# From unit 4 on, V is the stationary operand and P, divided by its sums first, the moving one

## Chip, cores and metric

One core of a Trainium2 chip. The metric is device time in microseconds (us), the median over runs of the whole kernel. Engines: PE is TensorE (PEld its weight load, which overlaps), DVE VectorE, ACT ScalarE, POOL GpSimd, SP the queue that issues nearly all DMAs.

## What is computed

Attention over 4 batches, 8 heads, 768 positions of 64 values, with a bias by head, in which a row sees the first `n_global` columns and the `n_local` before it. Its output, 3072 rows of 512, goes through a feed-forward layer of 2048 (512 to 2048 to 512).

```python
scores = scale * q @ k.T + bias          # bias = -slope[head] * distance
a = exp(where(keep, scores, -1e9) - max)
a = a / (sum(a) + 1e-9)
x = a @ v                                # heads side by side: 3072 x 512
h = x @ w_in
g = maximum(h, 0) + alpha * minimum(h, 0)
out = g @ w_out
```

## The kernel before

The work is cut into 12 units (`NU`) of 256 positions, three to a batch, `c = u % 3` being the place in the batch; each unit has two tiles of 128 rows, `t`. A row sees at most 192 kept columns (its own 128 and the ones before, or the first 32), held in 64-column groups `g`; for the first unit of a batch (`c = 0`) one group of tile 0 is missing ("gap").

From unit 2 on, products in fp16 are made of a high and a low half, three products for one. For one head:

- `split_pair` (L756) loads q and k of two heads and splits them; `load_pair` (L772) puts the score products of two heads in one PE operation, of four heads (`wide = 4`) from unit 4 (`QUAD`) on, in the PSUM buffers sp and av. They are products of 64 rows by 64 columns of the array, four of which stand side by side (`scores_of`, L687).
- `attend` (L803): DVE adds the bias and takes the maximum (L831), ACT takes the exponential and its row sums (L843), POOL and DVE form the sums' inverse for a group of `GROUP[u]` heads (L856, L859). P, not yet divided, is scaled and split into ps, high half on ACT (L385, by `mul`), low half on DVE (L412, by `rest`), each for all 384 columns at once; SP transposes it by DMA into pt (L890).
- `values` (L906): P transposed is the stationary operand, V the moving one, 64x64 by 64 columns; 36 such products a head (27 where `c = 0`), all heads of a group in one PE operation (L925). The result, rows by head columns in PSUM, is multiplied by the inverse sums on DVE into xn (L936).
- `pieces` (L941), from unit 4 on: three sums and differences of quarters of xn (L953), a high and a low half of each piece in xs (L397, L411), and four DMA transposes on SP into xt (L967). `seven` (L1074) makes the hidden layer of two blocks from seven products instead of eight (L1108); `ff_out` (L1154) makes the output products (L1170). Units 0 to 3 use `ff_in` (L1010) with whole weights.

All operations go to `Plan` (L150) with a key, the place in a common order (16 keys to a unit from unit 2 on), and estimated costs; a list scheduler picks for each engine the ready operation of lowest key, and the order it finds is the program's. So each engine works in a fixed order, and PE waits at an operation until every operand of it is there. The constants at L314 to L363 set keys (`LEAD`: how many keys ahead of its hidden layer a unit's attention begins; `F1`, `W0`: first loads), estimated costs (`SLOW`, `SHARE`, `BLOCK`) and buffer counts (`sp=2, av=2, h=2, o=2` are the eight PSUM banks).

Of the kernel before, what the change touches and what calls it, by code (L numbers as in the profile page):

```python
# [15 lines left out]
F16 = mybir.dt.float16  # L16
# [8 lines left out]
P = 128  # L25
# [22 lines left out]
def lay_out(q, k, v, n_global, n_local, moe_w_in, moe_w_out, moe_alpha):  # L48
# [5 lines left out]
    qk = np.zeros((NU, 4, P, 672), q.dtype)  # L54
    for u in range(NU):
        b, c = divmod(u, 3)
        cols = list(range(256 * c, 256 * c + 128)) + list(range(GL))
        cols += list(range(256 * c + 128, 256 * c + 256))
        if c:
            cols = list(range(256 * c - LOC, 256 * c)) + list(range(GL)) + cols  # L60
        n = 256 + len(cols)
        both = np.concatenate([qt[b, :, :, 256 * c : 256 * c + 256], kt[b][:, :, cols]], axis=2)
        qk[u, :, :, :n] = both.transpose(1, 0, 2).reshape(4, P, n)

    def groups(u, which):
# [3 lines left out]
        for t in range(2):  # L69
            at = 256 * c + 128 * t  # L70
            sets = (range(at - LOC, at - GL), list(range(at - GL, at)) + list(range(GL)), range(at, at + 64),
                    range(at + 64, at + 128))
            for n, g in enumerate(which):
                if at or g > 1:
                    out[64 * t : 64 * t + 64, n] = vn[b][list(sets[g])]
# [16 lines left out]
            [qk[0, :, :, :544], v0[:, :, 2:].reshape(P, 4, 260).transpose(1, 0, 2)], axis=2),  # L92
        "in_far0_dram": cont(v0[64:, :, :2].reshape(64, 2, 520).transpose(1, 0, 2)),
        "in_qk_dram": cont(qk[1:]),
        "in_first1v_dram": cont(groups(1, range(4)).transpose(0, 2, 1, 3).reshape(P, 2, 1024).transpose(1, 0, 2)),
        "in_far2_dram": cont(groups(2, (0, 1)).reshape(P, 1024)),
        "in_own_dram": cont(np.stack([groups(u, (2, 3)).reshape(P, 1024) for u in range(NU)])),
# [218 lines left out]
LEAD = 22  # L316
# [5 lines left out]
DP = 3.5  # L322
FLEX = {'ACT': 1.5, 'DVE': 2, 'POOL': 1}
GROUP = (4, 4, 2, 4, 4)
# [13 lines left out]
F1, F1S, W0, W0S = -60, 1, -61, 2  # L338
# [13 lines left out]
SHARE = 0.25  # L352
SLOW, SLOWER = 1.09, 1.04
V1S, V1M, V1R = 5.5, 2.5, 1
STEP4 = 1.5
# [10 lines left out]
def fast(tc, cn, a):  # L366
    nc = tc.nc
    ctx = ExitStack()
    with ctx:
# [64 lines left out]
        def build_bias(key):  # L434
# [7 lines left out]
            def columns():  # L442
                kw = dict(allow_small_or_imprecise_dtypes=True)
                nc.gpsimd.iota(rel.t[:, 0:LOC], pattern=[[-1, LOC]], base=LOC, channel_multiplier=1, **kw)
                nc.gpsimd.iota(rel.t[:, LOC:P], pattern=[[0, GL]], base=0, channel_multiplier=0, **kw)
                nc.gpsimd.iota(rel.t[:, P : 2 * P], pattern=[[-1, P]], base=0, channel_multiplier=1, **kw)
                nc.gpsimd.iota(j.t[:, 0:P], pattern=[[1, P]], base=0, channel_multiplier=0, **kw)

                nc.gpsimd.affine_select(out=rel.t[:, P : 2 * P], in_=rel.t[:, P : 2 * P], pattern=[[-1, P]],
# [967 lines left out]
```

## Time and profile before

| | |
|---|---|
| median of 3 runs | 609.06 us (605.25 to 611.16) |
| profiled execution | 601.96 us |
| its span | 600.2 us |
| mean granted clock of TensorE | 0.995 |
| PE busy | 570.6 us (95%) |
| DVE busy | 481.7 us (80%) |
| ACT busy | 406.9 us (68%) |
| POOL busy | 78.6 us (13%) |

The profile is one execution. The span is from its first to its last instruction. Busy times overlap across engines; a wait is put down to the operand that came last, and "issue" means that the engine waited for nothing that the profile shows. A wait that names an engine long done was for another thing, often a DMA.

### The profile page before, as it was taken

The page shows a single profiled execution, that of the slowest core. Times are in us where ns is not written, and L with a number is a line of the kernel's source. Part 1 is how long each engine was busy: PE and PEld are TensorE (multiplying, and loading weights), DVE is VectorE, ACT ScalarE, POOL GpSimd, SP SyncE. Part 2 cuts the span into 40 slices and gives each one's busy share as a digit, 9 for nine tenths or more (in the row PEclk, how much of TensorE's full clock was granted, in tenths as well). Part 3 has the DMA queues.
Part 4 walks back from the last instruction along what each step waited for, and adds up shares of the span by engine and source line. Part 5 has one row for each costly group of instructions (what it writes and reads, how often), then busy time and mean ns, then how long its engine had stood idle before and what let it go on. Part 6 is the DMA issues. An engine that isn't in the chain of part 4 may idle for free.

```text
span 600.2 us, 21524 instructions
## 1 busy us (share of the span) xinstructions
PE 570.6 (95%) x8844; PEld 408.7 (68%) x8844; DVE 481.7 (80%) x1368; ACT 406.9 (68%) x1053; POOL 78.6 (13%) x161
## 2 busy tenths in 40 slices
PE   7789999999999998989999898999999989989995
PEld 5667666666667676767767676777777767767783
DVE  6899999998896896789699497799698778676532
ACT  7899999988797689468477378577467556431321
POOL 2002333333333330000000000001000001000000
PEclk9899999999999999999999999999999999999999
DMA  8995786265565597498798697589798684422001
GB/s 277 409 406 205 195 224 195 44 133 141 118 142 108 133 250 166 101 192 175 183 181 185 134 202 140 119 207 182 157 212 132 128 189 67 90 43 24 36 2 41
DMA packets 123962, 94.04 MB, mean 157 GB/s; under 512 B 101712, under 2 KB 102480, under 8 KB 123856
## 3 DMA queue, kind: packets, MB, share of 16 engines
q1 hardware_dynamic: 123712, 92.46, 65.1%
q8 instruction: 71, 1.16, 0.8%
q14 instruction: 35, 0.29, 0.2%
q10 hardware_dynamic: 144, 0.13, 0.1%
HBM read 58.22 MB, written 6.29 MB: 107 GB/s over the span
## 4 chain that ended last, share of the span: by engine, by line
PE 76%; DVE 10%; DMA 7%; issue 3%; ACT 2%; SPq 1%; POOL 0%; DVEq 0%; ACTq 0%; POOLq 0%
PE o L1170 35%; PE ha L1108 13%; PE hc L1108 10%; PE h L1020 9%; PE av L918 5%; PE sp L696 3%; DMA xt<-xs 3%; DMA w<-in_w_dram 1%; DMA pt<-ps 1%; DMA first<-in_qk_dram 1%; DVE whl L412 1%; DVE pr L831 1%; DMA first<-in_first_dram 1%; DVE wf L604 1%; DVE g L1033 1%
## 5 line engine op out<-in xcount | busy, mean ns | idle before, releaser
L1170 PE MATMUL o<-whl,gh 128*128 128x512 f16 (+1 forms) x800 | 230.2, 371 | 0.0
L1170 PE MATMUL o<-whl,gl 128*128 128x512 f16 (+1 forms) x400 | 148.2, 371 | 1.9 <-DVE vdg L521 1.5
L1170 PEld LDWEIGHTS <-gh 128*128 128x128 f16 x800 | 71.6, 98 | 52.4 <-issue 2.3
L1108 PEld LDWEIGHTS <-sw 128*128 128x128 f16 x1536 | 91.5, 98 | 20.5 <-issue 7.3
L1020 PE MATMUL h<-xt,whl 128*128 128x256 f16 x768 | 92.3, 273 | 1.6 <-DVE g L1033 1.5
L1020 PEld LDWEIGHTS <-whl 128*128 128x128 f16 x768 | 74.4, 98 | 20.1 <-issue 2.6
L843 ACT ACTIVATE pr<-pr,sm 128x192 f32<-128x192 f32 (+1 forms) x176 | 77.1, 441 | 7.6 <-DVE sm L831 7.4
L1108 PEld LDWEIGHTS <-whl 128*128 128x128 f16 x1152 | 70.9, 98 | 14.0
L1170 PEld LDWEIGHTS <-gl 128*128 128x128 f16 x400 | 39.1, 98 | 45.2 <-DVE gl L1037 0.9
L411 POOL TENSOR_TENSOR gl<-g,gh 128x256 f16<-128x256 f32 x58 | 51.7, 892 | 115.0 <-ACT gh L1035 88.9
L831 DVE CUSTOM_DVE_ANT_0 pr<-sp,D 128x192 f32<-128x192 f32 (+1 forms) x192 | 58.6, 340 | 2.8 <-PE sp L696 2.5
L1108 PE MATMUL hc<-xt,sw 128*128 128x128 f16 x768 | 53.4, 219 | 4.3 <-DVE ga L1119 2.2
L1108 PE MATMUL ha<-xt,sw 128*128 128x128 f16 x768 | 53.4, 219 | 0.4 <-ACT u L1115 0.4
L1108 PE MATMUL ha<-xt,whl 128*128 128x128 f16 x768 | 53.3, 219 | 0.0
L412 DVE SCALAR_TENSOR_TENSOR ps<-pr,ps 128x384 f16<-128x384 f32 (+1 forms) x80 | 43.5, 544 | 6.9 <-ACT ps L385 6.7
L385 ACT ACTIVATE gh<-ga 128x512 f16<-128x512 f32 x32 | 20.2, 630 | 37.9 <-DVE ga L1147 37.8
L385 ACT ACTIVATE ps<-pr 128x384 f16<-128x384 f32 (+1 forms) x78 | 38.9, 502 | 2.5 <-DMA pt<-ps 2.3
L851 POOL TENSOR_TENSOR fin<-fin,sm 128x8 f32<-128x8 f32 (+1 forms) x22 | 8.4, 381 | 219.9 <-ACT pr L843 218.3
L385 ACT ACTIVATE g<-h,ak 128x256 f32<-128x256 f32 x59 | 27.6, 469 | 13.5 <-PE h L1020 9.4
L1115 ACT COPY u<-ha 128x256 f32<-128x256 f32 x32 | 11.8, 369 | 34.0 <-DVE ga L1119 33.7
L843 ACT ACTIVATION_READ_ACCUMULATOR pr<-pr,sm 128x1 f32 x176 | 33.8, 192 | 0.0
L412 DVE SCALAR_TENSOR_TENSOR x<-raw,x 128x672 f16<-128x672 f32 (+1 forms) x40 | 33.5, 843 | 0.0
(152 smaller groups left out, 930.8 us busy)
## 6 DMA issues: line engine op xcount, KB each, us to landing
w<-in_w_dram SPq DMA_DIRECT2D x32, 512.0 KB, 8.5
again<-in_w_dram SPq DMA_DIRECT2D x32, 512.0 KB, 4.8
raw<-in_qk_dram SPq DMA_DIRECT2D x28, 336.0 KB, 3.4
out_dram<-os SPq DMA_DIRECT2D x23, 256.0 KB, 2.6
rawv<-in_own_dram SPq DMA_DIRECT2D x10, 512.0 KB, 4.7
raw<-in_qk_dram SPq DMA_DIRECT2D x12, 272.0 KB, 3.6
gp<-v SPq DMA_DIRECT2D x48, 64.0 KB, 2.2
vr<-in_own_dram SPq DMA_DIRECT2D x3, 512.0 KB, 5.2
```

The costliest lines, as they stand in the source:

```text
L385: lambda: nc.scalar.mul(out=out(), in_=src(), mul=by.t if tile_ else by)),
L411: return e.tensor_tensor(out=out(), in0=src(), in1=hi(), op=ALU.subtract)
L412: return e.scalar_tensor_tensor(out=out(), in0=src(), scalar=val(), in1=hi(), op0=ALU.mult, op1=ALU.subtract)
L696: nc.tensor.matmul(out[i].t[64 * part : 64 * part + 64, 192 * t + 64 * g : 192 * t + 192], lhsT=q_[:, at : at + 64], rhs=k_[:, lo : lo + 1 ...
L831: op("DVE", key, c_dve(n) + 10, lambda t=t, g=g, n=n, dc=dc: v.tensor_tensor_reduce(out=seen_(t, g), in0=three(sp.t[:, 192 * t + 64 * g : ...
L843: op("ACT", key + 1, c_act(n, ptr=1) + 93, lambda t=t, g=g: nc.scalar.activation(out=seen_(t, g), in_=seen_(t, g), func=AF.Exp, bias=sm.t[ ...
L851: op("POOL", key + 3, c_pool(2 * G), lambda: nc.gpsimd.tensor_tensor(out=fin.t[:, : 2 * G], in0=fin.t[:, : 2 * G], in1=sm.t[:, 2 * G : 4 * ...
L918: nc.tensor.matmul(av[t].t[64 * part : 64 * part + 64, wide * n_ : wide * n_ + wide], lhsT=p_[:, 64 * part : 64 * part + 64], rhs=v_, star ...
L1020: nc.tensor.matmul(hp.t, lhsT=w.t[:, wi, wc], rhs=x.t[:, NC * xi + c, :], start=n == 0, stop=n == 3 * NC - 1)
L1108: nc.tensor.matmul(out, lhsT=weight(name, f, wi, c), rhs=x.t[:, 8 * piece + m * xi + 2 * j + c, :], start=start and p == n == 0, stop=n == ...
L1115: plan.op(key + k - SOON, r, w, ("ACT", c_act(256, True), lambda: nc.scalar.copy(out=out(), in_=src())), ("DVE", c_dve(256), lambda: v.ten ...
L1170: nc.tensor.matmul(o.t[:, cols], lhsT=g_()[:, tok], rhs=w.t[:, wi, 512 + cols.start : 512 + cols.stop], start=f == 0 and n == 0, stop=f == ...
```

## The change

From unit 4 (`TURN`) on:

- Scores are made for two heads at a time (`wide` is 2 there), and one PE operation holds the value products of an earlier pair and the score products of this one: the value products are kept in `waiting` until two pairs (`DEPTH`) are behind.
- P is divided by its sums before the product: the sums are made for each two heads at key + 1.5 (`SUMAT`), and both halves of P are made by tile `t` with a scalar for each row, so that there are two instructions of 192 columns (128 in the gap's tile) in place of one of 384.
- V is the stationary operand and P transposed the moving one. The columns of k, V and the bias are put in another order so that two groups of V meet 128 columns of P: of the 24 products a head, half have 128 columns and half 64. The result is x transposed, two heads by 64 dimensions on the partitions, in two PSUM banks (xb) held for the whole unit.
- `pieces` copies xb to xn on ACT, forms the same sums, and writes the halves straight into xt. Its four DMA transposes and the multiplication after the values go.

Also: groups are of two heads in units 0, 1 and 3 (four before); unit 3 splits all 384 columns of P; loads of unit 1 come before the first weights (`F1`); several keys and estimated costs move.

```diff
-LEAD = 22
+LEAD = 25
...
-DP = 3.5
+DP = 4
...
-GROUP = (4, 4, 2, 4, 4)
+GROUP = (2, 2, 2, 2, 2)
+TURN, SUMAT, LASTAT, DEPTH, XLATE, LEAD4 = 4, 1.5, 4, 2, 5, 22
...
-F1, F1S, W0, W0S = -60, 1, -61, 2
+F1, F1S, W0, W0S = -65, 1, -61, 2
...
-SHARE = 0.25
-SLOW, SLOWER = 1.09, 1.04
+SHARE = 0.3
+SLOW, SLOWER = 1.06, 1.04
...
-STEP4 = 1.5
+STEP4 = 2
...
-            wide = 4 if u >= QUAD else 2
+            wide = 4 if QUAD <= u < TURN else 2
...
+            before = waiting.pop(0) if len(waiting) >= DEPTH else None
+            if before:
+                op("PE", key, cost + before[0], lambda: (before[1](), scores()), r=xs + before[2], w=sps + before[3])
+            else:
+                op("PE", key, cost, scores, r=xs, w=sps)
...
+        def turned(u, h, key, sm):
...
+                for t, _, m, _ in windows(u):
+                    n = 64 * m
...
+                    by = lambda i=i, t=t: sm.t[:, 12 + 2 * i + t : 13 + 2 * i + t]
...
+                    plan.op(k, r, [(ps, (0, t))],
+                            ("ACT", c_act(n, ptr=1), lambda hi=hi, src=src, by=by: nc.scalar.mul(out=hi(), in_=src(), mul=by())),
...
+                    plan.op(k, r + [(ps, (0, t))], [(ps, (1, t))],
+                            ("DVE", Two(c_dve(n, False, 1)), lambda hi=hi, lo=lo, src=src, by=by: v.scalar_tensor_tensor(
+                                out=lo(), in0=src(), scalar=by(), in1=hi(), op0=ALU.mult, op1=ALU.subtract)))
...
+            def values():
+                sides = ((0, 0), (0, 1), (1, 0))
+                for s, (p_, v_) in enumerate(sides):
+                    for g in (1, 2, 0, 3):
+                        for t in range(2):
...
+                            for i in range(2):
+                                q = pts[i].t[64 * t : 64 * t + 64, p_]
+                                lo, hi = 64 * (g == 0), P - 64 * (g == 3)
+                                out = x[t].t[64 * i : 64 * i + 64, 64 * h + lo : 64 * h + hi]
...
+                                nc.tensor.matmul(out, lhsT=side(t, g, v_, i), rhs=q, start=s == 0 and g == 1,
+                                                 stop=s == 2 and g == (3 if whole else 0), skip_group_check=True)
+
+            waiting.append((3 * (2 * 57 + 2 * 33) + 100, values, [*pts, *used], [(x[0], h), (x[1], h)]))
+            if (u, h) == (NU - 1, H - 2):
+                while waiting:
+                    cost, fn, r, w = waiting.pop(0)
+                    op("PE", key + LASTAT - 3 * len(waiting), cost, fn, r=r, w=w)
...
         def pieces(u, y, key):
...
+                for t in range(2):
+                    mul(key - 0.05, lambda t=t: xn[u].t[:, t], lambda t=t: xb[u][t].t, 1 / PSC, [xb[u][t]], [(xn[u], t)],
+                        "ACT", 512, True)
...
+                if turn:
+                    part = lambda s, p=p, m=m: y.t[:, 8 * p + m * s // 2 : 8 * p + m * (s + 1) // 2, :].rearrange("p c t -> p (c t)")
+                    hi, lo = (lambda part=part: part(0)), (lambda part=part: part(1))
+                    copy(k, hi, src, [read], [(y, (p, 0))], n, XENG[0])
+                    rest(k, lo, src, None, hi, [read, (y, (p, 0))], [(y, (p, 1))], n, XENG[1], u <= XPOOL)
+                    continue
```

## Rows read from the trace of the kernel before

**Rows 1.** The page: each engine's busy time and count; below it the fetch queue.

```profile
PE 570.6 (95%) x8844; PEld 408.7 (68%) x8844; DVE 481.7 (80%) x1368; ACT 406.9 (68%) x1053; POOL 78.6 (13%) x161
...
q8 instruction: 71, 1.16, 0.8%
```

**Rows 2.** Busy time by stretch: start:end length, each engine's us (count), clock, DMA share.

```profile
45.00:90.00 45.00, 44.48 (x410) 29.52 (x409) 44.77 (x103) 43.33 (x96) 15.91 (x18) 1.00 0.71 208
...
224.00:268.00 44.00, 39.99 (x778) 29.78 (x777) 32.86 (x106) 31.02 (x89) 2.62 (x8) 1.00 0.74 155
...
sum 306.00, PE 294.54 PEld 213.78 DVE 243.16 ACT 196.51 POOL 11.93; mean PE 42.08 PEld 30.54 DVE 34.74 ACT 28.07 POOL 1.70
```

**Rows 3.** What TensorE waited for, 224 us to the end: total, times, longest.

```profile
PE av L918 <- issue: 3.5, 3, 1.7
...
PE hc L1108 <- issue: 2.1, 1, 2.1
PE sp L696 <- issue: 1.7, 1, 1.7
```

**Rows 4.** The same view, 45 to 224 us.

```profile
PE h L1020 <- DVE g L1033: 1.5, 3, 0.5
```

**Rows 5.** TensorE in order of time: start, us, line, [idle before, releaser].

```profile
239.50 0.38 PE L1170 MATMUL o<-whl,gl 128*128 128x512 f16 x1 [1.46 <-DVE vdg L521]
...
267.05 0.83 PE L1108 MATMUL hc<-xt,sw 128*128 128x128 f16 x12 [1.60 <-DVE ga L1119]
...
486.30 1.06 PE L696 MATMUL sp<-x 64*64 64x192 f16 x41 [1.69 <-issue]
```

**Rows 6.** Chain of work, 64-row bursts: start, us, line, count of products.

```profile
79.86 0.73 PE av L918 x72
...
82.64 0.62 PE sp L696 x24
...
225.00 1.11 PE sp L696 x48
...
280.77 1.25 PE av L918 x101
...
327.48 1.38 PE av L918 x144
...
345.04 1.31 PE av L918 x144
...
411.38 0.95 PE sp L696 x48
```

**Rows 7.** The same chain: the longest transfers of x.

```profile
256.81 9.40 DMA xt<-xs
...
300.73 7.22 DMA xt<-xs
```

**Rows 8.** Groups by line, 224 us on: count | busy us, mean ns | idle before.

```profile
L843 ACT ACTIVATE pr<-pr,sm 128x192 f32<-128x192 f32 x88 | 39.2, 447 | 4.4 <-DVE sm L831 4.4
...
L412 DVE SCALAR_TENSOR_TENSOR ps<-pr,ps 128x384 f16<-128x384 f32 x38 | 21.0, 552 | 3.5 <-ACT ps L385 3.5
...
L385 ACT ACTIVATE ps<-pr 128x384 f16<-128x384 f32 x37 | 19.0, 520 | 1.4 <-DMA pt<-ps 1.2
...
L1191 ACT ACTIVATE os<-o,osc 128x512 f32<-128x512 f32 x17 | 11.4, 686 | 6.5 <-PE o L1170 6.3
...
L936 DVE TENSOR_TENSOR xn<-av,sm 128x256 f32<-128x256 f32 x28 | 10.7, 420 | 13.7 <-PE av L918 13.6
...
L859 DVE RECIPROCAL sm<-sm 128x8 f32<-128x8 f32 x13 | 2.6, 197 | 0.0
```

**Rows 9.** The start: two transfers of the chain, and ScalarE's wait.

```profile
9.73 8.10 DMA w<-in_w_dram
17.85 7.41 DMA first<-in_qk_dram
...
16.59 0.78 ACT L597 ACTIVATE wb<-w 128x512 f16<-128x512 f32 x1 [2.02 <-DMA w<-in_w_dram]
```

More of the change, by code (lines that the diff above doesn't have):

```diff
@@ L70, in groups @@
             at = 256 * c + 128 * t
-            sets = (range(at - LOC, at - GL), list(range(at - GL, at)) + list(range(GL)), range(at, at + 64),
-                    range(at + 64, at + 128))
+            sets = falling(at, 4) + [range(GL)] + falling(at - LOC, 3)
             for n, g in enumerate(which):
-                if at or g > 1:
-                    out[64 * t : 64 * t + 64, n] = vn[b][list(sets[g])]
+                if at or g < 2:
+                    out[64 * t : 64 * t + 64, n] = vn[b][[x for y in sets[2 * g : 2 * g + 2] for x in y]]
         return out
@@ L456, in bias @@
                 for n, rows in enumerate(halves):
-                    seen_ = slice(64 * n, 64 * n + 192)
-                    v.tensor_tensor(out=d[rows, :192], in0=r[rows, seen_], in1=m[rows, seen_], op=ALU.max)
+                    taken = slice(64 - 64 * n, 256 - 64 * n)
+                    v.tensor_tensor(out=d[rows, :192], in0=r[rows, taken], in1=m[rows, taken], op=ALU.max)
                 v.tensor_scalar(out=g[:, P : 2 * P], in0=g[:, 0:P], scalar1=ngf, scalar2=BIG, op0=ALU.is_ge, op1=ALU.mult)
@@ L694, in scores_of @@
                             at = 128 * t + 64 * part
-                            lo = 256 + off + (0 if g else 64 * part)
-                            nc.tensor.matmul(out[i].t[64 * part : 64 * part + 64, 192 * t + 64 * g : 192 * t + 192],
-                                             lhsT=q_[:, at : at + 64], rhs=k_[:, lo : lo + 192 - 64 * g], start=j == 0, stop=j == n - 1)
+                            lo = 256 + off + (64 * (1 - part) if m == 3 else 0)
+                            nc.tensor.matmul(out[i].t[64 * part : 64 * part + 64, 192 * t : 192 * t + 64 * m],
+                                             lhsT=q_[:, at : at + 64], rhs=k_[:, lo : lo + 64 * m], start=j == 0, stop=j == n - 1)
         xn, xt_, xt, group = {}, {}, {}, {}
@@ L732, in move @@
             def move(i, to, first, src, j):
-                parts = [(j, 0), (j, 1)] if src is v16[u] or src is v16[u - 1] or u == 3 else [(j, 96)]
+                parts = [(j, 64)] if src is gp.get(u - 1) and u > 3 else [(j, 0), (j, 1)]
                 op("SP", key + 0.1 * i, c_dma(GL * 2048), lambda: nc.sync.dma_start(
@@ L786, in scores @@
                         x.t[64 * i : 64 * i + 64, sides[j][s]] for s in range(2)])
-            op("PE", key, 3 * 0.426 * (384 if u % 3 else 320) * wide / 2 + 200, scores, r=xs, w=sps)
+            cost = 3 * 0.426 * (384 if u % 3 else 320) * wide / 2 + 200
+            before = waiting.pop(0) if len(waiting) >= DEPTH else None
[3 more added lines that the diff above has]
+                op("PE", key, cost, scores, r=xs, w=sps)
         def score_pair(u, h, key):
@@ L805, in attend @@
             c = u % 3
-            gap = 0 if c else 64
-            npr = 384 - gap
-            plain = u < 2
+            plain, gap = u < 2, not c
             uh = f"{u}_{h}"
@@ L912, in values @@
                             for part in range(2):
-                                g = j + part if c or t else j + 1
-                                lo, hi = (0, 2) if c or t else (1, 1 + part)
+                                g = j + 1 - part if c or t else j
+                                lo, hi = (0, 2) if c or t else (1 - part, 1)
                                 if not lo <= j <= hi:
@@ L946, in pieces @@
             sums = (
[L947 to L950 removed]
+                (0, left, lambda: x(1, left), lambda: x(0, left), ALU.subtract, None),
```

193 lines of the change are left out of this document (120 added, 73 removed).

## The prediction

> **What bounds it now.** I read the page first: TensorE is busy 95% of the span [rows 1]. Then the busy times by stretch: from 224 to 530 us, where hidden products, output products and the attention of later units run together, TensorE is busy 294.54 of 306 us, while VectorE has a mean of 34.74 and ScalarE 28.07 in stretches of 44 us [rows 2]. So there only two things move the end: less work on TensorE, or fewer of the 11.5 us in which it stood still. The start is different: between 45 and 90 us TensorE, VectorE and ScalarE are all near full [rows 2], and before that the first loads stand in the chain [rows 9].
>
> Next the waits. From 224 us on TensorE waited 3.5 + 2.1 + 1.7 us for "issue", with longest pieces of 1.7 to 2.1 us [rows 3]; in order of time a further 1.46 us directly behind a value burst is put down to a VectorE instruction long done [rows 5], which I count with them: 8.8 us. From 45 to 224 us no such wait is listed [rows 4]. My reading is that these are instruction fetches. The fetch queue moved 71 packets [rows 1], and TensorE's 8844 products and 8844 loads make 249 instructions to a packet, so I give the queue to TensorE. A value burst of four heads is 144 products and 144 loads, 288 instructions, used up in 1.31 to 1.38 us [rows 6]; that is more than one packet holds, and two of the waits lie in or behind such bursts, one in a score burst that follows 2 us after one [rows 5]. The bursts of 216 instructions (`c = 0`) and 144 (unit 2) show none [rows 4, 6].
>
> The last cause: the chain has transposes of x that took 9.40 and 7.22 us [rows 7]; the first lands at 266.21 us, and the product at 267.05 us had stood 1.60 us for what follows from it [rows 5]. I count those 1.6 us.
>
> **The change, part by part.** *Products.* The value burst of 72 products takes 0.73 us and those of 144 take 1.345 on average, so one 64-column product costs (1.345 - 0.73)/72 = 8.5 ns and a burst 0.12 us besides. The score burst of 24 takes 0.62 us, of 48 1.11, so a 192-column product costs 20.4 ns; the burst of 48 of which half have 128 columns takes 0.95, so 128 columns cost 20.4 - 0.16/24 = 13.7 ns [rows 6]. A pair's values become 24 x 13.7 + 24 x 8.5 = 0.53 us, with its scores 1.15 us. A unit with `c > 0` goes from 2 x 1.345 + 2 x 1.11 = 4.91 to 4 x 1.15 = 4.60 us; with `c = 0` from 2 x 1.25 + 2 x 0.95 = 4.40 to 4 x 1.07 = 4.28 (the scores fall to 0.54, the values stay as long, since the quarter without a group only idles). Six units and two: -2.1 us. Bursts don't become fewer: four a unit before, of four heads each, and four of two heads now, plus two alone at the end and two more in unit 3. Each costs its 0.12 to 0.13 us and an entry that I put at no more than that; four at 0.2 is +0.8. Together -1.3 us. Bounds: were 128 columns as dear as 192, or as cheap as 64, the 32 pairs would differ by 24 x 6.7 ns or 24 x 5.2 ns each, so from +3.8 to -5.3.
>
> *Fetch.* The new burst has 72 products and as many loads: 144 instructions, fewer than a packet, as in unit 2's bursts that showed no wait [rows 4, 6]. The kernel loses 720 products of 8844. I let most of the 8.8 us go and leave one wait: -7.0. Bounds -8.8 and 0.
>
> *Transposes of x.* 32 DMA transposes leave SP's queue and the rings, and with them the wait behind the long one: -1.6 (bounds -1.6 and 0, if something else is late instead). What is late next is x itself: a unit's last values now stand five keys, about 14 us, ahead of its first hidden product; in them go two ScalarE copies at 0.69 us and twelve VectorE instructions at 0.42 to 0.69 us [rows 8], 6 to 10 us in all. That fits only while VectorE serves them soon.
>
> *P divided first.* Sixteen ScalarE halves a unit at the 0.447 us of the nearest row (192 columns with a row scalar), in place of eight at 0.520, and two copies at 0.686: +4.4 us a unit. VectorE: sixteen halves, between half of 0.552 and the whole of it, taken as 0.41, for eight at 0.552 is +2.1; four multiplications at 0.420 go, -1.7; two more reciprocals at 0.197, +0.4: +0.8 [rows 8]. TensorE's work hides both: ScalarE goes to 32.5 and VectorE to 35.5 of 44 us [rows 2]. POOL, busy 1.70 us of 44, takes its two added sums [rows 2]. Where the cover is gone, a late vector instruction stops TensorE as at 267.05 us. I allow +1.0 in all; bounds 0 and +6.4, a wait of 1.6 in every second unit.
>
> *The added wait.* A fused burst starts when q, k, the free score banks, V and the transposed P of the older pair are all there, and behind it in TensorE's order stand the hidden and output products. P has two pair steps, about 22 us, for exponentials, sums, halves and a transpose; even the 9.40 us transfer of rows 7 fits. Cost 0.
>
> *Start.* Loads of unit 1 pass ahead of the first weights. ScalarE's 2.02 us wait for those weights would be filled, but the weights come later, and the two transfers of 8.10 and 7.41 us only change places [rows 9]. Groups of two in units 0 and 1 add small VectorE instructions there. I take 0, between -2.0 and +2.0. The order of columns costs nothing: the instructions have the same sizes, apart from unit 3's gap.
>
> **Sum.** -1.3 - 7.0 - 1.6 + 1.0 = -8.9 us against the profiled 601.96, so 593.1. That execution is 7.1 us under the median of the runs shown, 609.06; I carry the difference over: 600.
>
> **Rivals.** *The issue waits stay.* Then only -1.3 - 1.6 + 1.0 = -1.9 remains: 607. For it speaks that the profile names no cause for them and that many bursts of 288 run without one; against it their length and place. [...]
>
> *Slower: the fused bursts wait for their latest operand.* With 34 of them, each standing d us, the gain is gone at d = 0.26, and the kernel is over 1% slower from (8.9 + 6.1)/34 = 0.44 us on; at 0.5 it gives 609 - 8.9 + 17 = 617. VectorE at 35.5 of 44 us speaks for it, the 22 us of lead against it.
>
> *The start gains too.* If unit 1's attention, begun earlier, fills ScalarE's idle 2.02 us and what follows from it, 600 - 2 to 600 - 5, with the last issue wait gone too: 595.
>
> **How the numbers follow.** Forecast 0.55, issue waits stay 0.25, fused bursts wait 0.1, start gains 0.1. The likeliest gives 600, alone 594 to 604. The range goes from 590 (every bound at its good end gives -5.3 - 8.8 - 1.6 - 2.0 = -17.7, 591) to 608, which holds the first rival and leaves out the slower one. About 1% (6 us) is what a measurement of this kernel can tell from no change. Faster by over 1%, under 603: most of the forecast and the start's case, 0.61. Within 1%: the rest of the forecast and the first rival, 0.30. Slower: 0.09.
>
> **What would show it.** Right: from 224 us on the "issue" waits fall from 7.3 us to under 2 and TensorE's idle time before 530 us from 11.5 to under 5; a fused burst takes 1.1 to 1.25 us; the counts fall by 720 products and 32 transposes; ScalarE gains some 4 us a unit. Wrong: issue waits of 1.5 us inside the short bursts, waits of TensorE for VectorE or ScalarE in most units, or hidden products starting later after unit 0.

## The result, and the profile after

| | before | after |
|---|---|---|
| median | 607.83 us (605.25 to 611.16, 4 runs) | 589.71 us (587.62 to 591.39, 4 runs) |
| profiled execution | 601.96 us | 589.39 us |
| its span | 600.2 us | 587.6 us |

The ratio is 0.970, with a 95% interval of 0.964 to 0.976: faster by 18 us. The forecast was 600, the range 590 to 608, so the median lies 0.3 us under the range's lower end. Side by side on another chip the two kernels took 604.41 us (11 runs) and 588.47 us (6 runs; ratio 0.975, 0.971 to 0.980), 16 us. The forecast gain was 8.9 us. Twice below, an execution over 1.5% longer than the fastest of its kernel is left out of a median.

The page of the kernel after, engines and fetch queue, beside [rows 1]:

```profile
PE 569.7 (97%) x8124; PEld 406.8 (69%) x8124; DVE 486.8 (83%) x1439; ACT 430.1 (73%) x1135; POOL 84.5 (14%) x198
...
q8 instruction: 65, 1.06, 0.8%
```

TensorE has the 720 products less that were forecast. It is busy for almost as long as before, but that sum does not price the products: the kernel before without its waits ("Both in the kernel before", below) shows 574.7 us with the same 8844 products. The gain shows as a share, 97 for 95%. The fetch queue moved 65 packets for 71.

The busy times from 224 to 530 us of the kernel after, as in [rows 2] (here as one stretch of 306 us, whose sum is to be held against that of before):

```profile
sum 306.00, PE 302.76 PEld 219.01 DVE 256.27 ACT 220.06 POOL 17.86; mean PE 302.76 PEld 219.01 DVE 256.27 ACT 220.06 POOL 17.86
```

TensorE stood still for 3.2 us where it had been 11.5. VectorE and ScalarE rose to 256.27 x 44/306 = 36.8 and 31.6 us of 44, from 35.0 and 28.3 (243.16 and 196.51 by the same factor).

What TensorE waited for in the kernel after, from 224 us to the end, beside [rows 3] (columns: total us, times, longest):

```profile
PE xb L1007 <- DMA pt<-ps: 1.1, 1, 1.1
PE ha L1201 <- DVE gb L1212: 0.7, 1, 0.7
PE o L1263 <- ACT os L1284: 0.6, 1, 0.6
PE ha L1201 <- ACT u L1208: 0.4, 1, 0.4
PE hc L1201 <- DVE ga L1212: 0.2, 1, 0.2
```

No wait for issue is left; three of the five are of under 0.65 us. Lines have moved: L1007 makes the values, L698 the scores, L1201 the products of seven, L1263 the output products.

The chain of work of the kernel after, one fused burst, beside [rows 6] (start, us, line, count of products):

```profile
457.30 0.65 PE xb L1007 x48
457.95 0.50 PE sp L698 x24
```

A pair's values and scores together take 1.15 us. Summed over all bursts of values and scores from 44 us on (from a burst's first product to the start of the next operation, without idle times of over 0.15 us), TensorE spends 49.2 us in the profile of [rows 1] and 46.3 us in this one. This sum is called burst time below.

Groups by line of the kernel after, from 224 us on, beside [rows 8] (count | busy us, mean ns | idle before):

```profile
L971 ACT ACTIVATE ps<-pr,sm 128x192 f16<-128x192 f32 x88 | 34.2, 445 | 3.7 <-DVE sm L866 2.7 <-ACT pr L849 0.6 <-ACT size L627 0.3
L975 DVE SCALAR_TENSOR_TENSOR ps<-pr,sm,ps 128x192 f16<-128x192 f32 x88 | 33.5, 413 | 1.0 <-ACT ps L971 0.9
```

The halves of P cost 445 and 413 ns, where the prediction had taken 447 and 410.

### The profile page after: what moved, and what is told of

The parts are those of the page before. It is cut to its first block, busy times and chain, and to the rows that moved or that the text cites. A ratio compares the mean times of both kernels' runs of the same rounds, so it can differ in the third digit from the quotient of the medians.

```text
span 587.6 us, 20213 instructions
## 1 busy us (share of the span) xinstructions
PE 569.7 (97%) x8124; PEld 406.8 (69%) x8124; DVE 486.8 (83%) x1439; ACT 430.1 (73%) x1135; POOL 84.5 (14%) x198
## 5 line engine op out<-in xcount | busy, mean ns | idle before, releaser
L1263 PE MATMUL o<-whl,gh 128*128 128x512 f16 (+1 forms) x800 | 230.4, 371 | 0.6 <-ACT os L1284 0.6
L1263 PE MATMUL o<-whl,gl 128*128 128x512 f16 (+1 forms) x400 | 148.2, 371 | 0.1
L1263 PEld LDWEIGHTS <-gh 128*128 128x128 f16 x800 | 71.0, 98 | 54.7 <-issue 1.3
L1201 PEld LDWEIGHTS <-sw 128*128 128x128 f16 x1536 | 92.4, 98 | 14.6 <-issue 1.3
L1201 PEld LDWEIGHTS <-whl 128*128 128x128 f16 x1152 | 71.1, 98 | 15.0 <-issue 1.0
L1263 PEld LDWEIGHTS <-gl 128*128 128x128 f16 x400 | 39.1, 98 | 44.4 <-POOL gl L412 0.6
L412 POOL TENSOR_TENSOR gl<-g,gh 128x256 f16<-128x256 f32 x58 | 50.4, 872 | 101.6 <-ACT gh L1128 78.9
L971 ACT ACTIVATE ps<-pr,sm 128x192 f16<-128x192 f32 (+1 forms) x128 | 47.8, 439 | 11.4 <-DVE sm L866 5.5
L1201 PE MATMUL ha<-xt,whl 128*128 128x128 f16 x768 | 53.2, 219 | 0.7 <-DVE gb L1212 0.7
L1201 PE MATMUL ha<-xt,sw 128*128 128x128 f16 x768 | 53.3, 219 | 0.5 <-ACT u L1208 0.4
L1201 PE MATMUL hc<-xt,sw 128*128 128x128 f16 x768 | 53.3, 219 | 0.3 <-DVE ga L1212 0.2
L975 DVE SCALAR_TENSOR_TENSOR ps<-pr,sm,ps 128x192 f16<-128x192 f32 (+1 forms) x128 | 48.1, 415 | 4.8 <-ACT ps L971 4.7
L863 POOL TENSOR_SCALAR sm<-sm 128x4 f32<-128x4 f32 x44 | 13.0, 295 | 246.4 <-ACT pr L849 245.6
L413 DVE SCALAR_TENSOR_TENSOR gl<-ga,gh 128x512 f16<-128x512 f32 x32 | 22.1, 690 | 13.8 <-ACT gh L386 13.8
L1128 ACT CAST gh<-g 128x256 f16<-128x256 f32 x64 | 25.4, 402 | 8.5 <-DVE g L1126 8.0
```

The source lines that it names most:

```text
L412: return e.tensor_tensor(out=out(), in0=src(), in1=hi(), op=ALU.subtract)
L413: return e.scalar_tensor_tensor(out=out(), in0=src(), scalar=val(), in1=hi(), op0=ALU.mult, op1=ALU.subtract)
L863: op("POOL", key + soon, c_pool(2 * G), lambda: nc.gpsimd.tensor_scalar(out=sm.t[:, 4 * G : 6 * G], in0=sm.t[:, 2 * G : 4 * G], scalar1=1e ...
L971: ("ACT", c_act(n, ptr=1), lambda hi=hi, src=src, by=by: nc.scalar.mul(out=hi(), in_=src(), mul=by())),
L975: ("DVE", Two(c_dve(n, False, 1)), lambda hi=hi, lo=lo, src=src, by=by: v.scalar_tensor_tensor(out=lo(), in0=src(), scalar=by(), in1=hi(), ...
L1128: op("ACT", key, c_act(UT), lambda: nc.scalar.copy(out=gh_(), in_=g_()), r=[rg], w=[rh])
```

## The experiments

The theory to begin with: the gain is the waits for issue, because the value bursts have become short. Its rival: something else is gone, the transposes of x above all, and the waits for issue go along with it. A median below is of 3 runs or more of the kernel named. The runs were made in five groups, each on a chip of its own, with the kernel before beside them: 605.65 us (second profile, short bursts, no transposes, longest bursts), 605.82 (both edits, narrow products, two pairs, two copies), 604.88 (third profile, three and four copies, all constants), 604.54 (single constants) and 604.41 (the kernel after again, two constants). So medians of different groups compare to within some 1.4 us. All 61 of these runs of the kernel before have a median of 605.33 us.

### The kernel before again

Two further profiles of the unchanged kernel, since the profiled execution of [rows 1] lay 7.1 us under its median.

> The kernel before, unchanged, looked at again, since its profiled execution (602 us) lies 6 us under the median of its runs while the changed kernel's does not. Fetch theory (TensorE stands still where a burst of small products uses up a packet of instructions faster than the next arrives; how many bursts meet it differs from run to run): TensorE's waits for issue from 224 us on are again 6 to 16 us, and the more of them, the longer the run: some 8.8 us at 602 us, 13 to 16 us at 607 to 611 us. Rival (the extra 6 us of the usual run are elsewhere, in the start or the clock): issue waits stay near 9 us whatever the time, and the stretch before 224 us or the granted clock differs.

> The kernel before, unchanged, for a third profile. If its waits vary from run to run, its profile has 15 to 18 us of TensorE waits over 0.2 us from 44 us on where the time is near the median of 605.8 or over it, and 12 to 14 where it is near 602; a stretch of half clock in the middle of the span shows only behind waits of about 2 us or more. If the difference between the first profile and the median lies elsewhere, the waits are the same and the start or the tail differs.

Medians 605.83 us (601.33 to 609.34, 10 runs) and 604.79 (602.62 to 609.57, 7). The profiled executions took 609.34 and 605.6 us.

TensorE's waits from 224 us on, first of the second profile:

```profile
PE hc L1108 <- DVE ga L1119: 3.9, 3, 2.0
PE sp L696 <- issue: 2.7, 1, 2.7
PE av L918 <- issue: 2.7, 2, 1.5
PE hc L1108 <- issue: 2.0, 1, 2.0
PE o L1170 <- DVE vdg L521: 1.5, 1, 1.5
```

And of the third:

```profile
PE av L918 <- issue: 3.6, 2, 1.8
PE sp L696 <- issue: 2.0, 1, 2.0
PE hc L1108 <- DVE ga L1119: 2.0, 2, 1.4
PE hc L1108 <- issue: 1.8, 1, 1.8
```

The waits for issue make the same sum each time, 7.4 us after 7.3 in [rows 3], whatever the run's time, as the rival of the second profile's forecast had it; a further one of 1.30 us stands at 42 us in the first profile, ahead of [rows 4], and one of 1.2 us between 40 and 170 us in the second. The product before which TensorE stood 1.69 us at 486.30 in [rows 5] stood 2.74 in the second profile. The waits put down to `ga` are 3.9 and 2.0 us. What the first profile had not shown is the clock. Busy times by stretch of the second profile (us of PE, PEld, DVE, ACT, POOL with counts; then TensorE's granted clock):

```profile
270.00:274.00 4.00, 4.00 (x28) 2.35 (x26) 3.86 (x11) 0.94 (x2) 0.41 (x2) 0.57 1.04 231
274.00:278.00 4.00, 4.00 (x86) 3.03 (x84) 2.71 (x8) 2.49 (x6) 0.20 (x1) 1.00 0.93 218
...
492.00:496.00 4.00, 3.51 (x59) 3.23 (x59) 1.13 (x4) 1.20 (x3) 0.00 (x0) 0.57 1.15 189
```

And TensorE in order of time in the same profile (start, us, line, count, idle before and its releaser):

```profile
269.21 0.83 PE L1108 MATMUL hc<-xt,sw 128*128 128x128 f16 x12 [1.96 <-DVE ga L1119]
...
271.45 0.63 PE L1170 MATMUL o<-whl,gl 128*128 128x512 f16 x1
...
274.62 0.38 PE L1170 MATMUL o<-whl,gl 128*128 128x512 f16 x1
...
492.49 1.91 PE L696 MATMUL sp<-x 64*64 64x192 f16 x41 [2.74 <-issue]
```

Behind a wait of 1.96 us, and again behind one of 2.74 us, the granted clock is 0.57 over 4 us. The clock records of the first profile hold two levels, 1.00 and 0.50; by these it stood at 0.50 for 3.4 us of the 4, and an output product of 512 columns shows as 0.63 us in place of 0.38, one starting every 0.43 us in place of 0.22. A stretch of 3.4 us at half the clock does 1.7 us less work. From 224 to 530 us the clock is 0.99 in the second and the third profile and 1.00 in the first, which has no record of 0.50 between 21 us and the tail. So a wait can cost more than its length, and the first profile was a favourable one. Of the expectations for the third profile, the one on the stretches of half clock stays open: its 0.99 does not tell behind which of its waits, of up to 2.0 us, the clock fell. The one on the sum of waits fails: over 0.2 us and from 44 us on they add up to 16.1 us in the second profile, but to 13.7 in the third, a run at the median; the first had 12.8. The start differs too: in its first 45 us the first profile has one stretch of 3.4 us at half clock, and the second a granted clock of 0.92, some 7 us at half. The mean granted clock sums this up: 0.995 in the first profile, 0.989 over the 61 runs. Taken as one minus the clock, times the span, that is 2.8 and 6.4 us, and the first profile lies 3.4 us under the median of those runs.

**Where the waits for issue stand.** The traces also tell where these waits are. Count TensorE's instructions in the order of their start: products, loads and the 47 (kernel after: 44) other instructions of its queue. In the first profile TensorE waited over 0.15 us thirteen times after the first 40 us. Each of the six waits for issue, and the one of 1.46 us put down to `vdg`, stands at a count that leaves 194 or 195 when divided by 256; none of the other six does. In the kernel after none of the nine such waits does, and none is for issue. One of the seven, on the last product of a burst (columns as in [rows 5]):

```profile
374.18 0.19 PE L918 MATMUL av<-v,pt 64*64 64x64 f16 x1 [1.54 <-issue]
```

So these waits lie whole multiples of 256 instructions apart; 256 from one such count to the next are called a block below. The fetch queue moved one packet of 16 KB for each 250 or 251 counted instructions (71 for 17735, 65 for 16292), and the packets can be numbered against the blocks. At the seven places the block's packet had landed 1.2 to 1.6 us before TensorE went on. At the 58 boundaries without a wait in the first profile it had landed at least 1.8 us before, and 7.5 us in the median; at the 59 of the kernel after at least 2.2, and 7.4 in the median. A block's packet started in the median 0.7 us (kernel after: 0.2) after the boundary before it. The waits for issue are therefore read as waits for instructions, and with `vdg` they make 8.8, 8.9 and 9.2 us from 224 us on. In the first profile five of the seven stand behind blocks that were used up fast: without its wait a block passed in 1.05 to 2.63 us seven times after 40 us, and two of these seven brought no wait. In the kernel after the fastest block took 4.35 us. Speed is not all: the other two waits, at 42 and 486 us, stand behind blocks of 4.0 and 3.4 us. There the packet itself started late, 3.0 and 2.8 us after the boundary before it; why is not shown.

### Shorter value bursts in the kernel before

```diff
-GROUP = (4, 4, 2, 4, 4)
+GROUP = (4, 4, 2, 4, 2)
```

> The kernel before with value bursts of two heads from unit 4 on (GROUP 2 there): 72 products and 72 loads, 144 instructions, in place of 288; score bursts of four heads stay. Fetch theory: the issue waits from 224 us on fall under 3 us; 16 more bursts at 0.2 us cost 3.2 us and smaller VectorE steps a little; so 3 to 8 us faster than before, 600 to 605. Rival (the waits come from the load of the rings by the transposes of x, not from the length of a burst): the waits stay at 8 to 15 us and the time rises by 3 us to about 611.

599.36 us (597.60 to 600.56), ratio 0.988 (0.981 to 0.995): -6.3 us. TensorE's waits from 224 us on:

```profile
PE ha L1108 <- issue: 1.6, 1, 1.6
PE ha L1108 <- DVE gb L1119: 1.3, 1, 1.3
```

One wait for issue of 1.6 us is left of 7.3. P's exponentials and halves and the transposes of x are as before; the sums and the multiplication behind the values come for two heads as well, 46 more instructions on VectorE and 32 on POOL. The length of the value burst is what these waits hang on. The sixteen bursts more cost some 1 us: the burst time is 50.4 us, against 49.2 and 49.5 in the first and third profile of before.

### No transposes of x in the kernel before

This kernel leaves out the transposing itself: x goes into the hidden layer as it lies, with instructions of the same sizes.

```diff
-                s = buf("wb", f"xs{u}_{p}", [P, 2, n], F16)
-                copy(k, lambda s=s: s.t[:, 0, :], src, ...)
...
-                    nc.sync.dma_start(out=y.t[:, 8 * p : 8 * p + m, :], in_=s.t..., transpose=True)
+                copy(k, hi, src, [read], [(y, (p, 0))], n, XENG[0])
+                rest(k, lo, src, None, hi, [read, (y, (p, 0))], [(y, (p, 1))], n, XENG[1], u <= XPOOL)
```

> The kernel before without the DMA transposes of x from unit 4 on: the halves are written straight into xt, so x goes untransposed into the hidden layer there; all else, the long bursts too, stays. Fetch theory: the waits behind the transposes go (1.6 us by the prediction), the issue waits stay at 6 to 14 us; 2 to 4 us faster, 603 to 606. Rival (ring load makes the fetches late): the issue waits fall under 3 us as well, and the time falls by 10 us or more, to under 598.

599.32 us (596.66 to 600.29), ratio 0.987 (0.980 to 0.994): -6.3 us, more than the 2 to 4 of the first theory and less than the rival's 10. TensorE's waits from 224 us on:

```profile
PE av L918 <- issue: 5.3, 4, 1.8
PE sp L696 <- issue: 2.0, 2, 1.5
PE hc L1104 <- DVE ga L1115: 0.6, 1, 0.6
```

Waits for issue of 7.3 us are still there, so the transposes do not cause them. What has gone is most of the wait put down to `ga`, in truth for x, and the 1.5 to 1.8 us of an output product (`vdg`, 1.46 us in [rows 5]), which by its place in the first profile is counted with the waits for issue. Adding up TensorE's idle times of over 0.15 us from the first product of seven on gives 7.9 us, against 11.4, 13.4 and 12.3 in the three profiles of before; that is -4.5 of the 6.3 us, of which 1.7 are waits for issue (7.3 us, for 8.8 to 9.2 with `vdg`). The profile's granted clock is 1.00 from 45 to 530 us, but the mean granted clock of the four runs is 0.989, as in the kernel before beside them, so the clock does not account for the other 1.8 us; they stay open.

### Both in the kernel before

> The kernel before with both edits that won 6 us each alone: values of two pairs a burst instead of four from unit 4 on, and the halves of x written straight into xt, without the transposes by DMA (x is left untransposed). Theory (two separate losses, the waits for issue and the waits for x): they add, 605.7 - 6.3 - 6.3 = 593, and 3 to 4 us are left to the kernel after, which the cheaper products explain. Rival (either edit alone already takes away the same thing, the stretches of half clock that follow any long wait): 597 to 599.

593.43 us (592.66 to 594.05), ratio 0.978 (0.972 to 0.984): -12.4 us; the two losses add. TensorE's waits from 224 us on:

```profile
PE hc L1104 <- DVE ga L1115: 0.5, 1, 0.5
PE av L918 <- DMA pt<-ps: 0.2, 1, 0.2
```

With two edits and none of the new arrangement, TensorE is as good as without waits: from the first product of seven on it idles 0.7 us. Some 4 to 5 us are left to the kernel after. Its burst time is 4.2 us less (46.3 for 50.5), and the wait for issue near 42 us, 1.30 us in the first profile and 1.5 with short bursts alone, is gone.

### Longer bursts and narrower products in the kernel after

Three edits of the kernel after: products of 64 columns for all, and two pairs' values in one burst, both together and each alone.

```diff
-            before = waiting.pop(0) if len(waiting) >= DEPTH else None
+            before = [waiting.pop(0) for _ in range(2)] if len(waiting) > DEPTH else None
...
-                                nc.tensor.matmul(out, lhsT=side(t, g, v_, i), rhs=q, ...)
+                                for k in range(0, hi - lo, 64):
+                                    far = P * (g - 1) + 3 * k if whole and 0 < g < 3 else k
+                                    nc.tensor.matmul(out[:, k : k + 64], lhsT=side(t, g, v_, i), rhs=q[:, far : far + 64], ...)
```

Both, 336 products and loads a burst (in this kernel each half of a split product starts its sum anew, so one partial term of a block is missing from the output; the instructions and their sizes are the ones described):

> The changed kernel with its value products cut to 64 columns (36 a head as before) and the values of two pairs joined to the scores of one: every second burst has 144 + 24 products, 336 instructions. No transposes of x, V stationary, P divided first, as in the changed kernel. Fetch theory: the issue waits that the change removed come back, 5 us or more from 170 us on, and the time is 595 to 602. Rival (ring load): no issue waits over 2 us, and the time is 590 to 593, for the products' few tenths of a microsecond a unit alone.

The narrow products alone, 192 a burst:

> The kernel after, but each value product of 128 columns split into two of 64 (the first of a bank alone starts it), so that a pair's values are 72 products instead of 48 and a burst of a pair's values and scores is about 192 instructions a kind instead of 144. In the run with two pairs in a burst and 64-column products the values took 0.64 us a pair against 0.545: +0.095 for each of 32 pairs, +3.0 us. Theory (waits for issue come with bursts of about 288, not with these): 592.5, waits for issue under 1 us. Rival (the waits grow with the number of 64x64 instructions as such): 4 to 6 us of waits for issue as well, 597 to 599.

Two pairs alone, 240 in the longer of two bursts:

> The kernel after, but the values of two pairs are joined to one burst of scores (every second burst has scores alone): 48 + 48 + 48 products of 64x64 tiles with the wide products, and the next has its scores alone. Theory (long bursts run the instruction stream dry): 2 to 4 us of waits for issue return after unit 4 and the time is 591 to 594. Rival (waits came with narrow products of 64 columns, which run through faster than they can be fetched, whatever the burst's length): no waits, 588 to 590.5.

Both: 598.46 us (597.59 to 601.12), ratio 0.988 (0.981 to 0.995). Narrow: 591.35 (589.39 to 593.00), 0.976. Two pairs: 590.08 (588.47 to 593.11), 0.975. The waits of the first, from 224 us on:

```profile
PE sp L698 <- issue: 1.7, 1, 1.7
...
PE xb L1007 <- issue: 0.4, 1, 0.4
```

One of its long bursts, from the chain of work:

```profile
509.61 1.38 PE xb L1007 x110
510.99 0.52 PE sp L698 x23
```

Of the second:

```profile
PE ha L1201 <- issue: 0.4, 1, 0.4
PE hc L1201 <- issue: 0.3, 1, 0.3
```

Of the third:

```profile
PE hc L1202 <- DVE ga L1213: 1.1, 1, 1.1
...
PE sp L698 <- issue: 0.3, 1, 0.3
```

A wait for issue of over 1 us returns with 336 alone, and only 2.1 us in all, less than the 5 us that were expected; narrowness alone or 240 alone brings none to speak of. Yet the long burst is as dense as those of the kernel before: it passes in 1.90 us, 0.62 of them its 24 scores, so that its 288 value instructions take 1.28 us, where the kernel before took 1.31 to 1.38. So a long and dense burst alone does not bring the waits. That it also matters how the blocks of 256 fall on the bursts is an estimate, from the counts of the first profile; it is not shown for this kernel.

The first kernel is 10 us slower than the kernel after (588.47 us below, on another chip). Its burst time of 50.9 us accounts for 4.6 of them, and its waits of over 0.2 us from 44 us on are 6.4 us, where the two profiles of the kernel after have 3.6 and 1.9.

The narrow run also prices the wide products: its fused burst lasts 1.25 us, not 1.15, and its burst time is 3.4 us longer (49.7). Its median is 2.9 us over 588.47 and 1.6 over the 589.71 of the result, neither measured beside it, which bears that price out roughly. In the run with two pairs, a long burst takes 1.67 and one of scores alone 0.62 us, 2.29 in all, twice 1.15: a burst more or less costs nothing here.

### What a wait costs: seven waits put into the kernel after

```diff
+                    if name == "A11" and s == 0 and u > 4:
+                        d = held
+                        nc.tensor.matmul(bank.t, lhsT=d[:, :128], rhs=d, start=True, stop=True)
+                        for _ in range(2):
+                            v.tensor_copy(out=d, in_=bank.t)
+                        nc.tensor.matmul(bank.t[:, :64], lhsT=d[:, :128], rhs=d[:, :64], start=True, stop=True)
```

`held` is a tile of zeros; two copies, then three and four.

> The kernel after with one wait of TensorE put in per unit from unit 5 on (seven in all): before the first product of seven, a product of 512 columns of zeros into the same bank, two copies of the bank by VectorE into one SBUF tile, and a product of 64 columns that reads that tile. TensorE then stands for VectorE's backlog and two copies of about 0.55 us, 1.5 to 2.5 us each. If a wait costs its own length and the two products (0.25 us): 7 x 2.25 = 15.8, 605.5. If each wait also pulls the granted clock down for a stretch of 3.4 us, as behind the two longest waits of the kernel before: 1.7 us more each, up to 617, and the windows behind the waits show the lower clock.

> The same with three copies, waits of about 2.05 us. If a wait costs its own length: 600.5 + 7 x 0.55 = 604.3. If some of these bring a stretch of half clock too: up to 616; the share of the seven that do is read from the windows.

> The run with seven added waits, with four copies in place of two, so that each wait grows from 1.51 to about 2.6 us. If a wait costs its own length: 600.5 + 7 x 1.1 = 608. If waits over about 2 us also bring a stretch of half clock of 3.4 us, as behind the waits of 1.96 and 2.74 us in the second profile of the kernel before: up to 1.7 us more each, 620, with the lower granted clock in the windows behind them.

The waits put in, from the list of waits of each (two, three and four copies):

```profile
PE ha L1203 <- DVE held L1202: 10.6, 7, 1.5
```

```profile
PE ha L1203 <- DVE held L1202: 15.7, 7, 2.2
```

```profile
PE ha L1203 <- DVE held L1202: 20.7, 7, 3.0
```

Medians 600.48 us (598.69 to 601.07, 8 runs), 609.54 (606.21 to 612.15, 10) and 612.61 (610.91 to 616.34, 3). The kernel after took 588.47; the waits and the two added products (0.25 us a place, 1.75 in all) give 600.8, 605.9 and 610.9. The first is met to 0.3 us: waits of 1.51 us (not 2, as the forecast of 605.5 had them) cost their length, and TensorE's granted clock is 1.00 from 230 to 530 us and 0.998 over the span. The other two are 3.6 and 1.7 us over. The mean granted clock of the runs is 0.993, 0.985 and 0.986; one minus the clock, times the span, is 4.1, 9.4 and 8.6 us, which is more than enough for the excess. Busy times by stretch in the run with three copies (clock in the third column from the end):

```profile
365.00:368.00 3.00, 3.00 (x40) 2.29 (x38) 1.87 (x7) 3.00 (x12) 0.38 (x2) 1.00 0.27 74
...
411.00:415.00 4.00, 3.87 (x29) 3.05 (x30) 3.66 (x13) 1.49 (x7) 0.00 (x0) 0.57 1.32 183
...
507.00:511.00 4.00, 4.00 (x31) 3.16 (x32) 2.10 (x9) 2.68 (x9) 0.00 (x0) 0.59 0.00 0
```

Two of its seven waits are followed by a clock of 0.57 and 0.59 over 4 us, which is 3.4 and 3.3 us at half, and the stretch from 365 us shows 1.00; this execution took 607.78 us, 1.9 over the sum. In the profile with four copies there is one such stretch for seven waits, 0.57 from 270 to 274 us, with 1.00 from 230 to 270 and from 274 to 530; that execution was the lowest of its runs, at 610.91 us, the sum itself. Which waits are followed so, the runs do not tell.

### The constants

The kernel after with the planner's constants of the kernel before, together (`STEP4` stays 2) and one by one:

```diff
-LEAD = 25
+LEAD = 22
-DP = 4
+DP = 3.5
-F1, F1S, W0, W0S = -65, 1, -61, 2
+F1, F1S, W0, W0S = -60, 1, -61, 2
-SHARE = 0.3
-SLOW, SLOWER = 1.06, 1.04
+SHARE = 0.25
+SLOW, SLOWER = 1.09, 1.04
```

> The kernel after with the planner's constants of the kernel before where they build: LEAD 22, DP 3.5, F1 -60, SHARE 0.25, SLOW 1.09 (STEP4 stays 2). Theory (the constants only fit the order to the new durations; the gain is the waits and the products): 588 to 592, as the kernel after. Rival (a good part of the gain, above all at the start, is the new order): 593 to 597.

> The kernel after with LEAD alone put back to 22 (attention of units 5 to 11 begins three keys later). If the shorter lead is what makes seven wait for x from unit 5 on (0.9, 0.6, 0.6 and 0.5 us of waits in the run with all constants back): 592 to 594. If not: 588.5 to 591.

> The kernel after with SHARE 0.25 and SLOW 1.09 put back, by which the planner estimates vector instructions beside POOL's and all of the first 34 keys. They change the order alone. If the order of VectorE's and ScalarE's work is what the six microseconds are: 592 to 595. If not: 588.5 to 591. If no one of the four constants brings over 2 us alone, the six are the sum of several small waits.

> The kernel after with DP alone put back to 3.5 (output products of units 0 and 1 half a key earlier). The run with all constants put back has a wait of 1.8 us of an output product at 49.0 us for a half of g from POOL, and its product 48 of ff_in starts at 49.9 instead of 46.8 us. If DP is the cause of the start's share: 591.5 to 593. If not: 588.5 to 591.

> The kernel after with F1 alone put back to -60, so that the loads of unit 1 stand behind the first weights again. The prediction took this edit as 0, between -2 and +2. If the loads' order is the start's share: 591 to 593. If not: 588.5 to 591.

All: 596.03 us (595.43 to 596.82), ratio 0.985 (0.977 to 0.993). `LEAD`: 593.26 (592.53 to 593.78). `SHARE` and `SLOW`: 592.97 (590.56 to 594.30). `DP`: 588.99 (588.19 to 591.23). `F1`: 588.71 (588.29 to 589.52). TensorE's waits from 44 us on, with all of them back:

```profile
PE o L1263 <- POOL gl L412: 1.8, 1, 1.8
...
PE hc L1201 <- DVE xt L412: 0.9, 1, 0.9
```

With `LEAD` alone:

```profile
PE hc L1201 <- DVE xt L412: 1.1, 2, 0.9
PE hc L1201 <- ACT gb L1208: 1.0, 3, 0.4
```

With `SHARE` and `SLOW`:

```profile
PE xb L1007 <- DMA pt<-ps: 1.8, 2, 1.4
...
PE hc L1201 <- DVE xt L412: 1.2, 1, 1.2
```

Neither `DP` nor `F1` matters alone. The other two cost some 4 us each (against 588.71 and 588.99 of the same group), and all of them together 7.6 against 588.47, on another chip; by the kernel before beside each it is 7.1. They don't add work; the order that they lead to leaves TensorE waiting for x, for P transposed or for a kept sum, in many small pieces. Over 0.2 us and from 44 us on its waits are 7.4, 6.2 and 6.8 us in these three profiles, against 3.6 and 1.9 in the two of the kernel after. So the new arrangement pays some 7 us for vector work that comes late unless the order is fitted to it, and the change contains the fit. No run puts the new constants into the kernel before, so it is not shown that they would win nothing there.

### The kernel after again, and with DP and F1 back

> The kernel after, unchanged, on the same chip as the experiments, with a second profile: 588 to 591, so that the single constants put back can be read against it. If its chip alone had made it fast: over 592.

> The kernel after with DP 3.5 and F1 -60 put back together. Each alone took 588.7 to 589.0. If the waits behind 270 us in the kernel after (1.1 us for the transposed P, 0.6 us for a stored output) go and nothing else comes: 587 to 589. If the two edits belong together: 590 to 592, with waits of the start as in the run with all constants back.

588.47 us (586.27 to 590.84, 6 runs), and 591.32 (589.22 to 592.48, 6 runs), both on a chip that no other experiment ran on. The two constants that did nothing alone cost 2.9 us together, in an order with two waits for P transposed (1.7 us) and with a start that is 2.9 us longer up to the first product of seven. Some 2 of the 2.9 us may be the clock alone: the mean granted clock is 0.990 for 0.993, and in the profiled executions 0.989 for 0.996. Whether the order brings that about is not shown. No kernel of these runs beats the kernel after. Its second profile, TensorE's waits from 44 us on:

```profile
PE o L1263 <- ACT os L1284: 0.5, 1, 0.5
PE ha L1201 <- ACT p L1208: 0.4, 1, 0.4
```

## Why the prediction was right and wrong

The direction and the main mechanism were right; the size was half of what came.

**Fetch, -7.0: right, and so is its cause.** Shorter bursts alone gave -6.3, and no wait for issue is left. That these are instruction fetches, a reading in the prediction, is borne out by their places in the first profile, seven of seven a multiple of 256 instructions apart, and by the packets that landed 1.2 to 1.6 us before their ends; counting the wait put down to `vdg` among them was right as well. One more, of 1.3 us at 42 us, lay ahead of the rows that the prediction looked at. The rival in which the waits for issue stay, 607, fell.

**Transposes of x, -1.6: the term that was mis-sized.** Alone they gave -6.3, 4.7 us more. The prediction took the one wait behind the longest transfer and called 1.6 its bound. The three profiles of before show 2.0 to 3.9 us for that kind, and without the transposes 1.7 us of waits for issue went too, 7.3 us for 8.8 to 9.2; why is not shown. 1.8 us of the 6.3 stay open. The bound was drawn from one wait in one execution.

**The clock: a step that was missing.** Every wait was priced at its length. Seven of 1.51 us cost that, to 0.3 us in all; behind some of 2.0 to 2.7 us the clock of 0.57 over 4 us cost 1.7 us more. The first profile had no such stretch in its middle (1.00 from 224 to 530 us), so its rows could not show it; the second and third did (0.99). By the mean granted clock it is some 2 us of the gain: one minus the clock, times the span, is 6.4 us over the runs of the kernel before and 3.9 to 4.9 over the two sets of runs of the kernel after.

**The difference carried over, +7.1: wrong.** 593.1 was the sum against the profiled execution, and 600 came of adding the distance to the median. Of that distance 3.7 us were chance: the median of the three runs shown, 609.06, lies that much over the 605.33 of the 61 later runs. The other 3.4 go with the first profile's good clock (2.8 us lost by it, for 6.4), and the change takes part of what the usual run loses. So of the 10.3 us between forecast and result, 3.7 are a starting point that was too high. The other 6.6 are gain that was missed: against 605.33 us the change wins 15.6, where 8.9 were forecast, and x alone makes 4.7 of the difference.

**Products, -1.3: undersized.** The fused burst is 1.15 us, as forecast, by parts a little off: a 128-column product took 15.2 ns and a 64-column one 7.5 (forecast 13.7 and 8.5). Six units at 4.91 to 4.60 and two at 4.40 to 4.27 make -2.1. The 0.8 us set aside for more bursts did not come: in the run with two pairs a burst more costs nothing, and with short value bursts sixteen more cost some 1 us. The burst time fell by some 3 us (49.2 and 49.5 to 46.3 and 46.2). It would have been 50.5 with two-head bursts in the old form, so the new arrangement of the products is worth 4.2 us to a kernel that has short bursts already. With -12.4 for the two edits, -4.2 for this, -1.5 for the wait at 43 us and +0.7 to +2.4 for the kernel after's own waits, the sum is -15.7 to -17.4 for the 16 to 18 measured.

**P divided first, +1.0: right for the order given.** From the first product of seven on TensorE idles 3.1 and 1.4 us in the two profiles of the kernel after, where the kernel before with both edits idles 0.7. ScalarE gained 3.3 us of 44 (4.4 forecast) and VectorE 1.9 (0.8 forecast). With the constants of before some 7 us come on top, more than the upper bound of 6.4: the late vector instruction that the prediction named is real, though those runs do not separate P's division from the sums of x. The prediction priced the lead through the five keys of x, and the cost estimates not at all.

**The added wait, 0, and the start, 0: right.** One fused burst waited for P transposed, 1.1 us in the first profile, and none in the second. The first product of seven starts at 225.5 and 224.6 us, against 224.2 to 226.2 in the kernel before. `F1` alone is worth 0.2 us.

## What to carry to other kernels

Seven added waits of 1.51 us cost their length here, and two of seven of 2.24 us were followed by a clock of 0.57 and 0.59 over 4 us, worth 1.7 us each; look at more than one execution before pricing a wait, and don't carry a profile's distance from the median of a few runs over to the forecast. Read waits without a releaser by their distance in instructions: here seven of seven lay multiples of 256 apart, which pointed at the instruction stream, and its packets, landed 1.2 to 1.6 us before, bore it out. Here value bursts of 288 products and loads had 7.3 us of waits for issue from 224 us on, and bursts of 144 with larger work between them 1.6 us, for 6.3 us of the time. When a change lets one engine's work lie later, fit the order to it before judging it: here some 7 of the 16 us won hang on it.

## What was not expected of the hardware

- In the first profile of the kernel before, TensorE stood still at 7 of 65 counts a multiple of 256 instructions apart after the first 40 us, each time until 1.2 to 1.6 us after the packet of the fetch queue for it had landed. Seven blocks passed in 1.05 to 2.63 us there, and waits for issue with `vdg` were 8.8 to 9.2 us from 224 us on in its three profiles; with no block under 4.35 us, in the kernel after, there were none at 59 counts.
- The granted clock was 0.57 to 0.59 over 4 us, about 3.4 us at half, behind waits of TensorE of 1.96 and 2.74 us in the second profile of the kernel before, where it was busy 293.76 of 306 us; behind 2 of 7 waits of 2.24 us, once for 7 of 2.96 and not at all for 7 of 1.51 in the kernel after.
- 288 products and loads of 64x64 tiles in 1.31 to 1.38 us went with 7.3 us of waits for issue from 224 us on; 288 in 1.28 us, in bursts of 336, with 2.1; 240, 192 or 144 in the kernel after with 0.7 or less.
- Products of 64x64 tiles took 7.5 ns with 64 columns and 15.2 with 128, in fused bursts of 144 instructions. With 192 columns a product cost 20.6 ns (24 in 0.62 us, 48 in 1.12), and a burst 0.1 us besides.
